# Transposing the last segment on TensorE, and the first input tile in two column parts

## The chip, the cores and the metric

The kernel runs on one core of one Trainium2 chip. The metric is the device time of one execution in microseconds (us), lower is better. A core has five engines that run their own instruction streams in order: PE (TensorE, matmuls and transposes), DVE (VectorE), ACT (ScalarE), POOL (GpSimd) and SP (SyncE, here only a queue that issues transfers). DMA transfers are issued from SP and ACT.

## The reference

The input `x` is 2048 tokens by 640. It is normalized per token, and two branches are computed from the normalized `xn` and combined.

```python
xn = _layernorm(x, axis=-1)
# attention in 4 segments of 512 tokens, 32 heads of 20 columns
q, k, v = (xn @ wq), (xn @ wk), (xn @ wv)          # split in heads and segments
p = softmax(q_s @ k_s.T * scale + causal_mask)      # inside segment s
a_dot = p @ v_s
a_mem = (phi(q_s) @ M) / (phi(q_s) @ z + 1e-6)      # memory of the earlier segments
o = g * a_mem + (1 - g) * a_dot                     # g = sigmoid(beta), one per head
M, z = M + phi(k_s).T @ v_s, z + phi(k_s).sum()     # phi(t) = t + 1 if t > 0 else exp(t)
s = o @ wo
# gated unit
h = sigmoid(xn @ w_gate) * (xn @ w_up)
y = silu(h @ w_down)
out = x + s * y
```

## The kernel before, in words

Tokens are worked on in 4 segments of 512, each of four tiles of 128 tokens (index `j`). Columns come in five chunks of 128 (index `c`, `DC` = 5).

**Order.** The schedule is manual: each engine gets its instructions in the order in which the Python code emits them. A tile from a pool waits until the buffer it gets has been read for the last time. All matmul results other than the scores (`Sps`, four PSUM banks) and the attention sums (`Aps`, one bank) go through one PSUM pool, `ps_d`, of three buffers (line 98), which all helper functions share.

**The head (lines 138 to 186 and 548 to 587).** SP loads the first input tiles, `Wv`, `Wk`, `Wq`. PE runs 11 matmuls on zeros (`keep_warm`). POOL builds constants: the identity `ident` (line 153), ones in `KT` (line 158), then the head indicator `Ind` (lines 160 to 169, six instructions), which `bound_k` (line 290) reads. For each of two pairs of tiles DVE takes statistics (`ln_stats`, lines 203 and 204), POOL turns the variance into a reciprocal root (`ln_rstd`, lines 207 and 208, tile `rs`), and DVE normalizes (`ln_norm`, line 212, tile `xn`). The statistics of both tiles of a pair come before their normalization on DVE. After that `late_constants` (line 174) gives POOL the rest of its constants behind a copy that waits for the fourth normalized tile: ones in `V`, and the block mask `BD`. Then each tile is transposed by PE (`ln_transpose`, line 226, five chunks into one PSUM tile `pT`) and copied by ACT into `xnT` (line 229). ACT issues the loads of `Wg` and `Wu` behind the first and second of these copies (line 573). Projections of V, K and Q follow.

**The middle.** For each unit of attention work PE does scores, ACT exponentials, and between them a planner fills in the rest: every item has a cost in ns, `due` grows by a fixed rate per unit, and `fill` emits items of the queue `dense` (gate, up and down products) until `done` reaches what is due. Items of one segment are planned for fixed slots of the units. Segments 0 to 2 get their attention output `odot` transposed through memory: a spill to `Od` (`out_spill`, line 417), then a DMA transpose to `oT` (line 422), then the output product in `out_mm`.

**The tail (lines 443 to 480 and 749 to 776).** The last segment has 21 units. In slot 18 `tail_spill` writes the first four column chunks of `odot` to memory, in slot 19 `tail_T` reads them back with a DMA transpose. Chunk five depends on the last head group; `tail_T4` transposes it on PE, two tiles at a time, with a copy on ACT (lines 457 and 458). The last attention block of a group is closed by `finalize` (lines 537 to 545, four DVE steps). Two of the eight down products of the last segment are held back (`held`): one is emitted before the last attention block (`held[1]`), one between the output products of tiles 0 and 1 (`held[0]`). A down product (`do_down`, line 409) is evacuated by ACT (tanh, line 412) and DVE (line 413). The eight output pieces are 320 columns wide each: `tail_mm` (line 466), then `tail_out` with a multiplication on DVE (line 473), an addition on POOL for tiles 0 and 1 and on DVE for 2 and 3, and a store.

Of the kernel before, what the change touches and what calls it, by code (L numbers as in the profile page):

```python
# [9 lines left out]
P = 128  # L10
D = 640
H = 32
DH = 20
E1 = DH + 1
NSEG = 4
L = 512
F = 1536
DC = D // P
# [4 lines left out]
HD = D // 2  # L23

BF = mybir.dt.bfloat16
F32 = mybir.dt.float32
ACT = mybir.ActivationFunctionType
ALU = mybir.AluOpType
# [47 lines left out]
def kernel(  # L76
# [14 lines left out]
    nc = tc.nc  # L91
    x2 = A_x.flatten_outer_dims()
    o2 = out.flatten_outer_dims()

    cpool = ctx.enter_context(tc.tile_pool(name="const", bufs=1))
    ps_s = ctx.enter_context(tc.tile_pool(name="ps_s", bufs=1, space=PSUM))
    ps_a = ctx.enter_context(tc.tile_pool(name="ps_a", bufs=1, space=PSUM))
    ps_d = ctx.enter_context(tc.tile_pool(name="ps_d", bufs=3, space=PSUM))
    lnp = ctx.enter_context(tc.tile_pool(name="ln", bufs=2))
# [4 lines left out]
    fpool = ctx.enter_context(tc.tile_pool(name="fpool", bufs=2))  # L104
    xpool = ctx.enter_context(tc.tile_pool(name="xpool", bufs=2))
# [4 lines left out]
    Od = [dpool.tile([L, D], BF, name=f"Od{i}") for i in range(2)]  # L110
# [7 lines left out]
    xt_of, xnT_of = {}, {}  # L118
# [14 lines left out]
    Wo = cpool.tile([P, DC, D], BF, name="Wo")  # L133
# [7 lines left out]
    for half in range(2):  # L141
        load_x(0, ((2 * half, 2 * half + 1), (2 * half + 1, 2 * half + 2)))
        hs = slice(half * HD, (half + 1) * HD)
# [12 lines left out]
    KT = cpool.tile([P, NG, L], BF, name="KT")  # L156
    QT = cpool.tile([P, NG, L], BF, name="QT")
    nc.gpsimd.memset(KT[:].bitcast(mybir.dt.uint32), 0x3F803F80)

    Ind = []  # L160
    for hb in range(2):
        t = cpool.tile([P, 3, 4, 4], F32, name=f"Ind{hb}")
        nc.gpsimd.memset(t[:], -1.0)
        base = 2 * hb * P - 16 * hb * DH
        nc.gpsimd.affine_select(out=t[:], in_=t[:], compare_op=ALU.is_ge, fill=0.0, base=base,
                                pattern=[[P, 3], [-DH, 4], [-4 * DH, 4]], channel_multiplier=1)
        nc.gpsimd.affine_select(out=t[:], in_=t[:], compare_op=ALU.is_ge, fill=0.0, base=DH - 1 - base,
                                pattern=[[-P, 3], [DH, 4], [4 * DH, 4]], channel_multiplier=-1)
        Ind.append(t)

    V = [cpool.tile([P, 4, H, E1], BF, name=f"V{i}") for i in range(2)]
    BD = cpool.tile([P, MOFF[-1]], BF, name="BD")
    Mbd = cpool.tile([P, MOFF[-1]], BF, name="Mbd")
    def late_constants(after):
        nc.gpsimd.tensor_copy(BD[:, 0:1], after[:, 0:1])
        for i in range(2):
            nc.gpsimd.memset(V[i][:, :, :, DH:E1], 1.0)
        nc.gpsimd.memset(BD[:], 1.0)
        for c, (h0, h1) in enumerate(HEADS):
            t = BD[:, MOFF[c]:MOFF[c + 1]].rearrange("p (h e) -> p h e", e=E1)  # L180
            nh, base = h1 - h0 + 1, P * c - DH * h0
            nc.gpsimd.affine_select(out=t, in_=t, compare_op=ALU.is_ge, fill=0.0, base=base,
                                    pattern=[[-DH, nh], [0, E1]], channel_multiplier=1)
            nc.gpsimd.affine_select(out=t, in_=t, compare_op=ALU.is_ge, fill=0.0, base=DH - 1 - base,
                                    pattern=[[DH, nh], [0, E1]], channel_multiplier=-1)
# [24 lines left out]
    def ln_norm(n, j, mv, rs):  # L210
        xn = lnp.tile([P, D], BF, name="xn", bufs=3)
        nc.vector.tensor_scalar(xn[:], xt_of[n][:, j, :], mv[:, j, 0:1], rs[:, j:j + 1],
                                op0=ALU.subtract, op1=ALU.mult)
        return xn
# [6 lines left out]
    def ln_transpose(n, j, xn, eng):  # L221
        if n not in xnT_of:
            xnT_of[n] = xpool.tile([P, DC, L], BF, name="xnT")
        pT = ps_d.tile([P, DC, P], BF, name="pT", tag="d")
        for c in range(DC):
            nc.tensor.transpose(pT[:, c, :], xn[:, c * P:(c + 1) * P], ident[:])
        dst = xnT_of[n][:, :, j * P:(j + 1) * P]
        if eng is nc.scalar:
            nc.scalar.copy(dst, pT[:])  # L229
        else:  # L230
            nc.vector.tensor_copy(dst, pT[:])
# [72 lines left out]
    def bound_dma(n, half, engs):  # L304
        cb = seg[n]["cb", half]
        for r in range(4):
            engs[r % len(engs)].dma_start(QT[32 * r + DH:32 * r + E1, 4 * half:4 * half + 4, :],
                                          cb[4 * r:4 * r + 4, :])
# [116 lines left out]
    def out_store(n, j):  # L425
        tt = 4 * n + j
        nc.sync.dma_start(o2[tt * P:(tt + 1) * P, :], xt_of[n][:, j, :])
# [15 lines left out]
    C4 = (DC - 1) * P  # L443
    tail = {}

    def tail_spill():
        nc.sync.dma_start(Od[(NSEG - 1) % 2][:, 0:C4].rearrange("(j p) d -> p j d", p=P),
                          seg[NSEG - 1]["odot"][:, :, 0:C4])

    def tail_T():  # L450
        tail["oT"] = fpool.tile([P, DC, L], BF, name="oT", bufs=1)
        nc.sync.dma_start_transpose(out=tail["oT"][:, 0:DC - 1, :], in_=Od[(NSEG - 1) % 2][:, 0:C4])

    def tail_T4(j0, j1):
        po = ps_d.tile([P, 2, P], BF, name="po", tag="d")
# [1 line left out]
            nc.tensor.transpose(po[:, j - j0, :], seg[NSEG - 1]["odot"][:, j, C4:D], ident[:])  # L457
        nc.scalar.copy(tail["oT"][:, DC - 1, j0 * P:j1 * P].rearrange("p (j t) -> p j t", t=P), po[:])

    def tail_mm(i, c0, c1):  # L460

        if c0 == 0:
            tail["sp", i] = ps_d.tile([P, HD], F32, name="sp", tag="d")
        j, hs = i // 2, slice((i % 2) * HD, (i % 2 + 1) * HD)
        for c in range(c0, c1):
            nc.tensor.matmul(tail["sp", i][:], lhsT=tail["oT"][:, c, j * P:(j + 1) * P], rhs=Wo[:, c, hs],  # L466
                             start=(c == 0), stop=(c == DC - 1), skip_group_check=True)

    def tail_out(i, eng):
        s = seg[NSEG - 1]  # L470
        j, hs = i // 2, slice((i % 2) * HD, (i % 2 + 1) * HD)
        aa, xr = s["aa"][j], xt_of[NSEG - 1][:, j, :]
        nc.vector.tensor_tensor(aa[:, hs], aa[:, hs], tail["sp", i][:], op=ALU.mult)
        if i >= 6:
            eng.tensor_tensor(xr[:, hs], aa[:, hs], xr[:, hs], op=ALU.add)
            t0 = (4 * NSEG - 1) * P
            nc.sync.dma_start(o2[t0:t0 + P, hs], xr[:, hs])
        elif i % 2:
            eng.tensor_tensor(xr, aa[:], xr, op=ALU.add)
            out_store(NSEG - 1, j)  # L480


    def scores(unit):
# [72 lines left out]
    new_seg(0)  # L556
    xns = {}

    def ln0(j):
        xns[j] = ln_norm(0, j, mv, rs)  # L560

    for pair in range(2):
        for j in (2 * pair, 2 * pair + 1):
            ln_stats(0, j, mv)
            ln_rstd(mv, rs, slice(j, j + 1))
        for j in (2 * pair, 2 * pair + 1):
            ln0(j)
    late_constants(xns[3])
    for j in range(4):
        ln_transpose(0, j, xns[j], nc.scalar)  # L570
        if j < 2:
            w, src = ((Wg, B_w_gate), (Wu, B_w_up))[j]
            load_w(nc.scalar, w, src)
        if j == 0:
            keep_warm(3)
        if j == 1:
            do_V(0, 0, 0, nc.scalar)
            do_V(0, 1, 0, nc.scalar)
        if j == 2:
            do_V(0, 0, 1, nc.scalar)  # L580
            do_V(0, 1, 1, nc.scalar)
            do_V(0, 2, 0, nc.scalar)
# [136 lines left out]
    def fill(want):  # L719
        nonlocal done  # L720
        while done < want and dense and (dense[0][0] < 0 or dense[0][0] in ready):
            _, c, fn = dense.popleft()
            fn()
            done += c
# [8 lines left out]
    for n in range(NSEG):  # L733
        if n >= 1:
            outq.append((n - 1, out_steps(n - 1)))
        for slot, unit in enumerate(units[n]):
            scores(unit)
            pt = exps(unit)
            due += rate
            items = plans[n].get(slot, [])  # L740
            run([it for it in items if it[0] < 600])
            fill(due - rate / 2)
            if pend is not None:
                attend(*pend)
            pend = (n, unit, pt)
            run([it for it in items if it[0] >= 600])
            if outq and downs[outq[0][0]] == 8 and slot >= 5:
                run(outq[0][1].popleft())
                if not outq[0][1]:
                    outq.popleft()  # L750
            if slot == 9:
                ready.add(n + 1)
            if n == NSEG - 1 and slot == len(units[n]) - 3:
                tail_spill()
            if n == NSEG - 1 and slot == len(units[n]) - 2:
                tail_T()
            fill(due)
        if n + 1 < NSEG:
            relayout(n + 1, 1, Kd, KT, nc.sync)
            relayout(n + 1, 1, Qd, QT, nc.sync)  # L760
            bound_dma(n + 1, 1, [nc.sync])
    fill(1e12)
    held[1][2]()
    tail_T4(0, 2)
    attend(*pend)
    for i in range(2):
        tail_mm(i, 0, DC)
        tail_out(i, nc.gpsimd)
    held[0][2]()
    for i in range(2, 4):  # L770
        tail_mm(i, 0, DC)
        tail_out(i, nc.gpsimd)
    tail_T4(2, 4)
    for i in range(4, 8):
        tail_mm(i, 0, DC)
        tail_out(i, nc.vector)

# [1 line left out]
_INS = ['A_x', 'A_wq', 'A_wk', 'A_wv', 'A_wo', 'A_beta', 'B_x', 'B_w_gate', 'B_w_up', 'B_w_down']  # L779
# [26 lines left out]
```

## Time and profile before

| | us |
|---|---|
| median of 3 runs | 343.83 (343.44 to 344.74) |
| the profiled execution | 343.83 |
| its span, first to last instruction | 342.0 |
| costliest group: exponentials on ACT, line 494 | 150.3 busy |
| down products on PE, line 409 | 57.5 busy |
| gate and up products on PE, lines 386 and 395 | 59.7 busy each |
| DMA, bytes moved | 36.45 MB, 107 GB/s mean |

Times in the trace count from the start of the span. The granted TensorE clock is 1.00 over the whole span. An engine's busy time is no measure of what a change is worth: what counts is the wait that ends last at each place, and the chain that ended last follows such waits back from the end. In a row of the timeline the brackets give the engine's idle time before the row and the instruction that ended it. Ends of PE rows are modelled, and rows of independent instructions on one engine can overlap a little.

### The profile page before, as it was taken

How to read it: one execution, taken by the hardware profiler on the slowest of the kernel's cores; microseconds unless marked ns; L12 is line 12 of the kernel's file. 1: busy time of each engine (PE TensorE's matmuls, PEld its weight loads, DVE VectorE, ACT ScalarE, POOL GpSimd, SP SyncE). 2: the span in 40 equal slices, each digit the busy share in tenths (PEclk: the TensorE clock that was granted, in tenths of full speed). 3: DMA queues.
4: the chain of work that ended last, by engine and by line, in shares of the span. 5: the costliest groups of instructions: out<-in, count | busy, mean ns of one | idle time of the engine just before them, and what ended most of it. 6: DMA issues, size and time to landing. Idle time of an engine off the chain costs nothing.

```text
span 342.0 us, 8196 instructions
## 1 busy us (share of the span) xinstructions
PE 333.2 (97%) x3370; PEld 183.6 (54%) x3370; DVE 220.8 (65%) x516; ACT 221.7 (65%) x218; POOL 100.9 (29%) x172
## 2 busy tenths in 40 slices
PE   7999999999999999999999999999999999999995
PEld 3544444665554455556566545556446655544763
DVE  5374374375776777797768875878765575553355
ACT  3523676677786766766786757767965766767620
POOL 6800225223222243223232432232233223232122
PEclk9999999999999999999999999999999999999999
DMA  7987783302246514213265325014144100000132
GB/s 217 378 324 214 147 281 138 80 2 84 86 142 133 154 32 134 55 67 105 74 185 157 79 77 98 21 65 143 37 108 132 27 21 21 20 21 2 58 68 77
DMA packets 51573, 36.45 MB, mean 107 GB/s; under 512 B 27344, under 2 KB 50256, under 8 KB 51536
## 3 DMA queue, kind: packets, MB, share of 16 engines
q1 hardware_dynamic: 50224, 32.00, 33.6%
q10 hardware_dynamic: 1312, 3.93, 2.9%
q8 instruction: 26, 0.43, 0.5%
q14 instruction: 11, 0.09, 0.1%
HBM read 17.05 MB, written 12.32 MB: 86 GB/s over the span
## 4 chain that ended last, share of the span: by engine, by line
PE 86%; DVE 6%; ACT 3%; issue 2%; POOL 2%; ACTq 0%; POOLq 0%
PE yp L409 16%; PE up L395 14%; PE gp L386 14%; PE psq L250 11%; PE Aps L516 9%; PE Sps L486 7%; PE psv L313 5%; PE sp L434 4%; PE am L370 2%; PE cps L299 2%; ACT pt L494 1%; PE dm L351 1%; PE sp L466 1%; ACT mn L330 1%; DVE hT L398 1%
## 5 line engine op out<-in xcount | busy, mean ns | idle before, releaser
L494 ACT ACTIVATE pt<-Sps 128x2048 bf16<-128x2048 f32 (+1 forms) x81 | 150.3, 1855 | 35.7 <-PE Sps L486 33.1
L496 POOL TENSOR_SCALAR_AFFINE_SELECT pt<-pt 128x512 bf16<-128x512 bf16 x128 | 81.5, 652 | 226.0 <-ACT pt L494 226.0
L395 PE MATMUL up<-xnT,Wu 128*128 128x512 bf16 x240 | 59.7, 379 | 1.1 <-ACT tg L389 0.9
L386 PE MATMUL gp<-xnT,Wg 128*128 128x512 bf16 x240 | 59.7, 379 | 0.2 <-ACT V_140 L318 0.2
L409 PE MATMUL yp<-Wd,hT 128*128 128x320 bf16 x384 | 57.5, 299 | 0.0
L398 DVE SCALAR_TENSOR_TENSOR hT<-tg,up 128x512 bf16<-128x512 bf16 x48 | 32.8, 683 | 36.6 <-PE up L395 26.9
L516 PEld LDWEIGHTS <-pt 128*128 128x128 bf16 x1280 | 42.7, 96 | 14.4 <-issue 3.0
L389 ACT ACTIVATE tg<-gp 128x512 bf16<-128x512 f32 x48 | 28.5, 594 | 26.1 <-PE gp L386 26.1
L409 PEld LDWEIGHTS <-hT 128*128 128x128 bf16 x384 | 35.3, 97 | 15.3 <-issue 2.6
L386 PEld LDWEIGHTS <-Wg 128*128 128x128 bf16 x240 | 21.4, 97 | 23.9 <-issue 3.4
L395 PEld LDWEIGHTS <-Wu 128*128 128x128 bf16 x240 | 21.1, 97 | 24.4 <-issue 4.3
L486 PE MATMUL Sps<-QT,KT 21*128 21x128 bf16 (+3 forms) x512 | 32.8, 301 | 0.5 <-ACT pt L494 0.5
L313 PE MATMUL psv<-Wv,xnT 128*128 128x320 bf16 x160 | 26.5, 299 | 0.5 <-DVE ktd L255 0.3
L250 PE MATMUL psq<-xnT,Wq 128*128 128x512 bf16 x100 | 24.3, 378 | 0.0
L250 PE MATMUL psq<-xnT,Wk 128*128 128x512 bf16 x100 | 24.3, 378 | 0.0
L486 PEld LDWEIGHTS <-KT 21*128 21x128 bf16 x512 | 9.7, 92 | 26.9 <-issue 26.4
L516 PE MATMUL Aps<-V_140,pt 128*128 128x21 bf16 x640 | 22.4, 173 | 0.0
L516 PE MATMUL Aps<-V_139,pt 128*128 128x21 bf16 x640 | 22.3, 173 | 0.0
L313 PEld LDWEIGHTS <-xnT 128*128 128x128 bf16 x160 | 15.3, 98 | 10.9 <-ACT xnT L229 0.9
L434 PE MATMUL sp<-Wo,oT 128*128 128x320 bf16 x120 | 20.2, 298 | 0.2 <-ACT tg L389 0.2
L255 DVE CAST ktd<-psq 128x512 bf16<-128x512 f32 x20 | 13.7, 684 | 6.3 <-PE psq L250 6.2
L436 DVE TENSOR_TENSOR aa<-aa,sp 128x320 bf16<-128x320 bf16 x24 | 11.6, 483 | 7.2 <-PE sp L434 7.2
(155 smaller groups left out, 325.4 us busy)
## 6 DMA issues: line engine op xcount, KB each, us to landing
Wg<-in_B_w_gate_dram ACTq DMA_DIRECT2D x1, 1920.0 KB
Wu<-in_B_w_up_dram ACTq DMA_DIRECT2D x1, 1920.0 KB
Wd<-in_B_w_down_dram SPq DMA_DIRECT2D x1, 1920.0 KB
KT<-Kd_92 SPq DMA_DIRECT2D x16, 80.0 KB
QT<-Qd_90 SPq DMA_DIRECT2D x16, 80.0 KB
Xd_95<-xn SPq DMA_DIRECT2D x8, 160.0 KB
KT<-Kd_93 SPq DMA_DIRECT2D x16, 80.0 KB
QT<-Qd_91 SPq DMA_DIRECT2D x16, 80.0 KB
```

Of the source, the lines that this page charges most:

```text
L250: nc.tensor.matmul(ps[:], lhsT=W[:, k, c * P:(c + 1) * P], rhs=xnT_of[n][:, k, :], start=(k == 0), stop=(k == DC - 1))
L313: nc.tensor.matmul(ps[:], lhsT=xnT_of[n][:, k, j * P:(j + 1) * P], rhs=Wv[:, k, half * HD:(half + 1) * HD], start=(k == 0), stop=(k == DC ...
L386: nc.tensor.matmul(gp[:], lhsT=Wg[:, k, f * P:(f + 1) * P], rhs=xnT_of[n][:, k, :], start=(k == 0), stop=(k == DC - 1))
L389: nc.scalar.activation(tg[:], gp[:], ACT.Tanh, scale=0.5)
L395: nc.tensor.matmul(up[:], lhsT=Wu[:, k, f * P:(f + 1) * P], rhs=xnT_of[n][:, k, :], start=(k == 0), stop=(k == DC - 1))
L398: nc.vector.scalar_tensor_tensor(out=h[:], in0=seg[n]["tg"][:], scalar=1.0, in1=up[:], op0=ALU.add, op1=ALU.mult)
L409: nc.tensor.matmul(yp[:], lhsT=s["hT"][f][:, j * P:(j + 1) * P], rhs=Wd[:, f, hs], start=(f == 0), stop=(f == FC - 1))
L434: nc.tensor.matmul(sp[:], lhsT=s["oT"][:, c, j * P:(j + 1) * P], rhs=Wo[:, c, hs], start=(c == 0), stop=(c == DC - 1))
L486: nc.tensor.matmul(Sps[:, r, c0:c0 + ncol], lhsT=KT[32 * r:32 * r + E1, g, kb * P:(kb + 1) * P], rhs=QT[32 * r:32 * r + E1, g, q0:L], star ...
L494: nc.scalar.activation(pt[:, :, 0:ntot], Sps[:, :, 0:ntot], ACT.Exp, scale=SCALE)
L496: nc.gpsimd.affine_select(out=pt[:, :, c0:c0 + P], in_=pt[:, :, c0:c0 + P], compare_op=ALU.is_ge, fill=0.0, base=0, pattern=[[0, 4], [1, P ...
L516: nc.tensor.matmul(acc["ps"][:, qb, r, :], lhsT=t[:, r, off:off + P], rhs=V[n % 2][:, kb, 4 * g + r, :], start=acc["fresh"], stop=True, sk ...
```

## The change

Four edits. Where the whole `Ind` block was built ahead of the first normalization, its six POOL instructions now stand in `late_constants`, behind the copy that waits for the fourth normalized tile. The first input tile is normalized in two column parts (384 and 256), and its transposes are emitted at once, before the second tile's normalization: three chunks copied by ACT, two copied by DVE. For the last segment the spill and the DMA transpose go; the new `tail_T` transposes the four chunks of one tile on PE into a `ps_d` tile and copies 512 columns on ACT (tiles 0 and 2) or DVE (tiles 1 and 3), emitted after the loop over the units and ahead of the held down product. The output pieces of the last tile are 384 and 256 columns wide.

```diff
-    Ind = []
-    for hb in range(2):
-        t = cpool.tile([P, 3, 4, 4], F32, name=f"Ind{hb}")
-        nc.gpsimd.memset(t[:], -1.0)
...
+    Ind = [cpool.tile([P, 3, 4, 4], F32, name=f"Ind{hb}") for hb in range(2)]
...
     def late_constants(after):
         nc.gpsimd.tensor_copy(BD[:, 0:1], after[:, 0:1])
+
+        for hb in range(2):
+            t = Ind[hb]
+            nc.gpsimd.memset(t[:], -1.0)
...
         for i in range(2):
             nc.gpsimd.memset(V[i][:, :, :, DH:E1], 1.0)
...
-    def tail_spill():
-        nc.sync.dma_start(Od[(NSEG - 1) % 2][:, 0:C4].rearrange("(j p) d -> p j d", p=P),
-                          seg[NSEG - 1]["odot"][:, :, 0:C4])
-
-    def tail_T():
-        tail["oT"] = fpool.tile([P, DC, L], BF, name="oT", bufs=1)
-        nc.sync.dma_start_transpose(out=tail["oT"][:, 0:DC - 1, :], in_=Od[(NSEG - 1) % 2][:, 0:C4])
+    def tail_T(j, eng):
+        if j == 0:
+            tail["oT"] = fpool.tile([P, DC, L], BF, name="oT", bufs=1)
+        po = ps_d.tile([P, DC - 1, P], BF, name="po", tag="d")
+        for c in range(DC - 1):
+            nc.tensor.transpose(po[:, c, :], seg[NSEG - 1]["odot"][:, j, c * P:(c + 1) * P], ident[:])
+        dst = tail["oT"][:, 0:DC - 1, j * P:(j + 1) * P]
+        if eng is nc.scalar:
+            nc.scalar.copy(dst, po[:])
+        else:
+            nc.vector.tensor_copy(dst, po[:])
...
+    def tail_piece(j, c0, c1, eng):
+
         s = seg[NSEG - 1]
+        sp = ps_d.tile([P, c1 - c0], F32, name="sp", tag="d")
+        for c in range(DC):
+            nc.tensor.matmul(sp[:], lhsT=tail["oT"][:, c, j * P:(j + 1) * P], rhs=Wo[:, c, c0:c1],
+                             start=(c == 0), stop=(c == DC - 1))
         aa, xr = s["aa"][j], xt_of[NSEG - 1][:, j, :]
+        nc.vector.tensor_tensor(aa[:, c0:c1], aa[:, c0:c1], sp[:], op=ALU.mult)
+        a0 = 0 if c1 == D and j < 3 else c0
+        if j == 3 or c1 == D:
+            eng.tensor_tensor(xr[:, a0:c1], aa[:, a0:c1], xr[:, a0:c1], op=ALU.add)
+            t0 = (4 * (NSEG - 1) + j) * P
+            nc.sync.dma_start(o2[t0:t0 + P, a0:c1], xr[:, a0:c1])
...
+    CA = 3 * P
+
     def ln0(j):
-        xns[j] = ln_norm(0, j, mv, rs)
+        if j:
+            xns[j] = ln_norm(0, j, mv, rs)
+            return
+        xns[0] = lnp.tile([P, D], BF, name="xn", bufs=3)
+        for cs in (slice(0, CA), slice(CA, D)):
+            nc.vector.tensor_scalar(xns[0][:, cs], xt_of[0][:, 0, cs], mv[:, 0, 0:1], rs[:, 0:1],
+                                    op0=ALU.subtract, op1=ALU.mult)
+
+    def first_transpose():
+        xnT_of[0] = xpool.tile([P, DC, L], BF, name="xnT")
+        for c0, c1 in ((0, 3), (3, 5)):
+            pT = ps_d.tile([P, c1 - c0, P], BF, name="pT", tag="d")
+            for c in range(c0, c1):
+                nc.tensor.transpose(pT[:, c - c0, :], xns[0][:, c * P:(c + 1) * P], ident[:])
+            dst = xnT_of[0][:, c0:c1, 0:P]
+            if c0:
+                nc.vector.tensor_copy(dst, pT[:])
+            else:
+                nc.scalar.copy(dst, pT[:])
...
         for j in (2 * pair, 2 * pair + 1):
             ln0(j)
+            if j == 0:
+                first_transpose()
     late_constants(xns[3])
     for j in range(4):
-        ln_transpose(0, j, xns[j], nc.scalar)
+        if j:
+            ln_transpose(0, j, xns[j], nc.scalar)
...
-            if n == NSEG - 1 and slot == len(units[n]) - 3:
-                tail_spill()
-            if n == NSEG - 1 and slot == len(units[n]) - 2:
-                tail_T()
             fill(due)
...
+    for j in range(4):
+        tail_T(j, nc.vector if j % 2 else nc.scalar)
     fill(1e12)
     held[1][2]()
     tail_T4(0, 2)
     attend(*pend)
...
+    tail_piece(0, 0, HD, nc.gpsimd)
+    tail_piece(0, HD, D, nc.gpsimd)
     held[0][2]()
...
+    tail_piece(2, 0, HD, nc.vector)
+    tail_piece(2, HD, D, nc.vector)
+    tail_piece(3, 0, 384, nc.vector)
+    tail_piece(3, 384, D, nc.vector)
```

The old loops over `tail_mm` and `tail_out` at the end go, and the new calls stand in their order: the two pieces of tile 0, the held product, tile 1, the transposes of chunk five for tiles 2 and 3, tile 2, tile 3.

More of the change, by code (lines that the diff above doesn't have):

```diff
@@ L158 @@
     nc.gpsimd.memset(KT[:].bitcast(mybir.dt.uint32), 0x3F803F80)
-    Ind = []
-    for hb in range(2):
-        t = cpool.tile([P, 3, 4, 4], F32, name=f"Ind{hb}")
-        nc.gpsimd.memset(t[:], -1.0)
[L164 to L169, printed above, removed]
+    Ind = [cpool.tile([P, 3, 4, 4], F32, name=f"Ind{hb}") for hb in range(2)]
     V = [cpool.tile([P, 4, H, E1], BF, name=f"V{i}") for i in range(2)]
@@ L175, in late_constants @@
         nc.gpsimd.tensor_copy(BD[:, 0:1], after[:, 0:1])
+        for hb in range(2):
+            t = Ind[hb]
+            nc.gpsimd.memset(t[:], -1.0)
+            base = 2 * hb * P - 16 * hb * DH
+            nc.gpsimd.affine_select(out=t[:], in_=t[:], compare_op=ALU.is_ge, fill=0.0, base=base,
+                                    pattern=[[P, 3], [-DH, 4], [-4 * DH, 4]], channel_multiplier=1)
+            nc.gpsimd.affine_select(out=t[:], in_=t[:], compare_op=ALU.is_ge, fill=0.0, base=DH - 1 - base,
+                                    pattern=[[-P, 3], [DH, 4], [4 * DH, 4]], channel_multiplier=-1)
         for i in range(2):
@@ L458, in tail_T4 @@
         nc.scalar.copy(tail["oT"][:, DC - 1, j0 * P:j1 * P].rearrange("p (j t) -> p j t", t=P), po[:])
[L460 to L469, printed above, removed]
+    def tail_piece(j, c0, c1, eng):
         s = seg[NSEG - 1]
-        j, hs = i // 2, slice((i % 2) * HD, (i % 2 + 1) * HD)
+        sp = ps_d.tile([P, c1 - c0], F32, name="sp", tag="d")
+        for c in range(DC):
+            nc.tensor.matmul(sp[:], lhsT=tail["oT"][:, c, j * P:(j + 1) * P], rhs=Wo[:, c, c0:c1],
+                             start=(c == 0), stop=(c == DC - 1))
         aa, xr = s["aa"][j], xt_of[NSEG - 1][:, j, :]
[L473 to L480, printed above, removed]
+        nc.vector.tensor_tensor(aa[:, c0:c1], aa[:, c0:c1], sp[:], op=ALU.mult)
[4 more added lines that the diff above has]
+            nc.sync.dma_start(o2[t0:t0 + P, a0:c1], xr[:, a0:c1])
     def scores(unit):
@@ L765 @@
     attend(*pend)
-    for i in range(2):
-        tail_mm(i, 0, DC)
-        tail_out(i, nc.gpsimd)
+    tail_piece(0, 0, HD, nc.gpsimd)
+    tail_piece(0, HD, D, nc.gpsimd)
     held[0][2]()
-    for i in range(2, 4):
-        tail_mm(i, 0, DC)
-        tail_out(i, nc.gpsimd)
+    tail_piece(1, 0, HD, nc.gpsimd)
+    tail_piece(1, HD, D, nc.gpsimd)
     tail_T4(2, 4)
-    for i in range(4, 8):
-        tail_mm(i, 0, DC)
-        tail_out(i, nc.vector)
+    tail_piece(2, 0, HD, nc.vector)
+    tail_piece(2, HD, D, nc.vector)
+    tail_piece(3, 0, 384, nc.vector)
+    tail_piece(3, 384, D, nc.vector)
 _INS = ['A_x', 'A_wq', 'A_wk', 'A_wv', 'A_wo', 'A_beta', 'B_x', 'B_w_gate', 'B_w_up', 'B_w_down']
```

## The prediction

> **What bounds the kernel now.** First the page: its first part and the chain that ended last.
>
> ```profile
> PE 333.2 (97%) x3370; PEld 183.6 (54%) x3370; DVE 220.8 (65%) x516; ACT 221.7 (65%) x218; POOL 100.9 (29%) x172
> ...
> PE 86%; DVE 6%; ACT 3%; issue 2%; POOL 2%; ACTq 0%; POOLq 0%
> ```
>
> PE (TensorE) holds 86% of the chain. The reader is to see that outside a short head and a short tail nothing is worth anything unless PE starts earlier, stalls longer or does more. So I read the timeline at both ends, in order of time: start, duration, engine, line, tile, idle time before it. First the head:
>
> ```profile
> 4.01 0.21 DVE L204 BATCH_NORM_AGGREGATE mv<-st 128x2 f32<-128x12 f32 x1
> ...
> 4.55 0.32 POOL L167 TENSOR_SCALAR_AFFINE_SELECT Ind_135<-Ind_135 128x48 f32<-128x48 f32 x1
> ...
> 4.85 0.23 POOL L207 TENSOR_SCALAR rs<-mv 128x1 f32<-128x1 f32 x1
> 5.00 0.21 DVE L204 BATCH_NORM_AGGREGATE mv<-st 128x2 f32<-128x12 f32 x1
> ...
> 5.78 0.45 DVE L212 TENSOR_SCALAR xn<-xt_111,mv,rs 128x640 bf16<-128x640 bf16 x1 [0.57 <-POOL rs L208]
> ...
> 6.70 0.45 DVE L212 TENSOR_SCALAR xn<-xt_111,mv,rs 128x640 bf16<-128x640 bf16 x1 [0.47 <-POOL rs L208]
> ...
> 9.69 0.45 PE L226 MATMUL pT<-ident,xn 128*128 128x128 bf16 x5 [0.39 <-DVE xn L212]
> ```
>
> The first tile's statistics end at 4.22, yet POOL takes up `rs` at 4.85, behind the head indicator `Ind`. VectorE (DVE) waits for `rs` twice (0.57 and 0.47 us), and each later DVE step follows. At 9.69 PE still waits for DVE; from there PE runs almost without a gap.
>
> Then the tail:
>
> ```profile
> 328.26 0.44 ACT L412 ACTIVATE t_5149<-yp 128x320 bf16<-128x320 f32 x1 [0.60 <-PE yp L409]
> ...
> 328.46 1.79 PE L409 MATMUL yp<-Wd,hT 128*128 128x320 bf16 x12
> 328.73 0.49 DVE L413 SCALAR_TENSOR_TENSOR aa<-t_5149,yp 128x320 bf16<-128x320 bf16 x1 [1.47 <-ACT t_5149 L412]
> 329.13 0.20 DVE L537 RECIPROCAL rd<-Aps 128x8 f32<-128x8 f32 x1
> ...
> 329.93 0.24 DVE L545 TENSOR_TENSOR odot<-odot,od 128x160 bf16<-128x160 bf16 x1
> ...
> 330.23 0.28 PE L457 MATMUL po<-ident,odot 128*128 128x128 bf16 x2
> ...
> 330.62 0.37 ACT L458 COPY oT<-po 128x256 bf16<-128x256 bf16 x1
> ```
>
> PE goes from one matmul group to the next and never waits for the transposed `oT`; the chain stays on PE until 336.70 and then on DVE until 339.24. DVE is occupied without a break from 328.73 to 330.17: evacuation of the sixth down product, then four steps of `finalize`.
>
> **What the Trainium skill says.** "PSUM — Partial Sum Buffer", "PSUM: the matmul accumulator": matmul results leave PE only through PSUM, in 2 KiB banks. So a PE transpose costs a buffer and a copy as well; the trace agrees (`po` and `pT` each have an ACT copy behind them). "TensorE: Matmul & The Clock Gate", "Wait — 56ns, not 53.3ns?": 55.6 ns start to start for 128 columns, warm. The trace agrees: five transposes last 0.45 us, two 0.28, so 0.057 each and 0.17 fixed. "VectorE: DVE Perf Modes", "The TRN2 errata" and "The perf-mode tier table": a copy out of PSUM takes 120 + columns/mode cycles at 0.96 GHz, and 16-bit data may go at up to 2 per cycle. The trace has the fp32 case only (512 columns 0.685 us against 0.658 by the formula) and no bf16 PSUM read on DVE.
>
> **The head.** Six POOL instructions of `Ind` (3.09 to 4.87, 1.78 us) go behind the copy at 10.86, ahead of the `V` and `BD` memsets. POOL's constants then end near 18.6 instead of 16.8; its next work is at 36.62. `Ind` is first read on DVE at 20.02 and 25.67 and would be built by about 12.7; `V` ones are read from 39.35. All hidden. If this cover were gone, DVE's `ik` would wait by the excess.
>
> First `rs`: in the second pair it takes 0.97 us from `mv` end (8.18) to ready (9.15). So 4.22 + 0.97 = 5.19; DVE is free at 5.21; norm starts about 5.23 instead of 5.78. In two parts it costs 0.31 to 0.38 and 0.25 to 0.35 (bounds: all of the 0.446 us row that is not a fixed 0.11 goes with columns, or fixed is 0.28), the second starting 0.08 before the first's end as independent DVE rows do: part two ends 5.71 to 5.88. Its two transposes (0.28, 0.05 after it) end at 6.04 to 6.21, behind part one's three, which end by 6.0. Now DVE's own copy of 256 columns stands in front of the second tile's norm: it starts at 6.08 to 6.25 and lasts 0.28 at 2 per cycle (256/2/0.96 + 150 ns) or 0.42 at 1. The second `rs` is ready at 5.21 + 0.97 = 6.18. So the second norm starts at 6.28 to 6.59 against 6.70: gain 0.1 to 0.4, I take 0.3. From there statistics, norms and transposes of tiles 3 and 4 follow on DVE with unchanged durations, so PE's 9.69 becomes about 9.4. The part-one copy on ACT (384 columns, 0.48 by ACT's 0.37 for 256 and 0.69 for 640) ends before `psv` needs it.
>
> ACT issues the `Wg` load behind its first copy, so about 0.8 us earlier (6.78 to 6.0); `Wu` follows. They share the DMA engines with `Wq`. By bytes moved per queue, SP's loads of x, Wv, Wk and Wq (3.1 MB) are in by about 15; 0.8 us earlier sharing could delay the end by about 1 us, and `Wq` is used at 17.68. Hidden: cost 0; without cover, the lateness beyond 17.4.
>
> **The tail.** Removed: a spill (issue 0.38 us) and a DMA transpose (2.40) on SP. The next SP work is the output at 334.50 and PE didn't wait for `oT`, so this gives nothing. Added: 16 transposes in four groups, each with a buffer of the three-deep pool and a 512-column copy, ACT, DVE, ACT, DVE. They stand on PE just ahead of the held down product that started at 328.46. By themselves 16 x 0.057 = 0.91 us.
>
> But the buffers: group 0 starts at 328.46, its ACT copy (512 columns, 0.585 as the fp32 row) runs 328.90 to 329.49. Group 1 starts at 328.69. Group 2 needs the sixth down product's buffer, free after DVE's 328.73 + 0.49 = 329.22: PE 329.27 to 329.67; ACT copy to 330.29. Group 3 takes group 0's buffer at 329.54. Group 1's copy waits on DVE behind `finalize`: start about 330.08, 0.42 us at 2 per cycle (512/2/0.96 + 150 ns), end 330.50. The fourth tile after it in the rotation, the held down product, starts at 330.55. Loss: 330.55 - 328.46 = 2.09 us. Behind the waiting matmul stand the rest of PE's program: last attention, all output products. These are in the old order, with group 3's copy (done by 331) and `finalize` before them, so nothing gives the loss back. A pause of this length does not slow PE: at 248.48 it resumed after 0.91 us idle with five matmuls in 1.24 as before.
>
> Price bounds: DVE copy at 1 per cycle 0.685, start 330.82, loss 2.36. If the buffer handed to the down product is group 2's, freed by ACT at 330.29, the loss is 1.88. The trace shows that the rotation isn't strict: at 224.65 a `psv` waits for a `ktd` copy and starts while the older `gp` is still being read until 225.01.
>
> The last output pieces become 384 and 256 columns instead of 320 twice. DVE's multiplications and additions cover the same 640 columns with the same counts, and DVE is what ends last there, so its end stays at 339.24 plus the shift. The last store is 64 KB instead of 80; 0 to 0.1 us gain out of 2.76 after 339.24, taken as 0.
>
> **Sum.** -0.3 + 2.09 = +1.79 us. The profiled execution took 343.83 with a span of 342.0 and 1.83 around it; its time equals the median of the three runs. Forecast 343.83 + 1.79 = 345.6.
>
> **Rivals.**
> 1. The down product gets the buffer freed by ACT: 1.88 - 0.35 = +1.5, 345.3, which is not slower by this study's bound (0.5%, 1.72 us, is about what a measurement can tell from no change, so slower begins at 345.55). It decides as soon as that buffer is free before 330.45. For it: ACT is idle from 328.70. Against: a strict rotation, which most groups show by never waiting, gives group 1's. 0.32.
> 2. DVE copies bf16 from PSUM at 1 per cycle, or the product gets group 3's buffer: +2.36 - 0.15 = +2.2, 346.0, up to 346.6 with group 3. For it: all PSUM rows on DVE run at 1. Against: the skill's tier table. 0.19.
> 3. The earlier `Wg` load makes `Wq` late enough to stall the projections: more than 2.7 us late is needed to cost anything; each further us adds one, 346.5. Against: the byte counts. 0.04.
> 4. PE gains more than the head shows, because buffers in the long middle fall otherwise; the trace's waits for buffers there sum to about 2 us. With all of them gone 343.6; beyond that nothing speaks for faster. 0.05.
>
> The forecast case has 0.40. Its own range is 345.1 to 346.0, slightly more of it above 345.55 than below. Slower: 0.23 of it, 0.19 of rival 2, 0.04 each of rivals 1 and 3: 0.50. Same: 0.17 + 0.28 + 0.01 = 0.46. Faster 0.04. Range for 8 in 10: 344.7 to 346.5.
>
> **What would show it.** Head: `rs` starts near 4.3, the second norm near 6.4, PE's third-tile transposes near 9.4. Tail: groups of four transposes near 328.2, a DVE copy of 512 columns of 0.42 behind `finalize`, and an idle time of about 0.6 us on PE ended by that copy before the seventh down product. Wrong if PE runs into that product without a gap, if the DVE copy comes ahead of `finalize`, or if the K and Q projections wait for DMA.

## The result and the profile after

The changed kernel takes 345.25 us (median of 6 runs, 345.0 to 345.53) against 343.86 for the kernel before (6 runs): +1.39 us, a ratio of 1.0038 with a 95% interval of 1.0025 to 1.0051. By the bound that the prediction names, 345.55 us, this counts as the same time and not as slower. The profiled execution took 345.33 us with a span of 343.5.

First the page of the changed kernel, busy times and the chain's shares by engine:

```profile
PE 334.4 (97%) x3386; PEld 184.5 (54%) x3386; DVE 222.7 (65%) x520; ACT 222.7 (65%) x220; POOL 100.3 (29%) x172
...
PE 87%; DVE 6%; ACT 4%; issue 2%; ACTq 0%
```

POOL, 2% of the chain before, has left it; ACT has grown from 3 to 4%. PE has 16 more instructions, the transposes. The page can't say what that is worth, so again both ends in order of time. The head of the changed kernel:

```profile
4.31 0.23 POOL L205 TENSOR_SCALAR rs<-mv 128x1 f32<-128x1 f32 x1 [1.16 <-DVE mv L202]
...
5.24 0.64 DVE L562 TENSOR_SCALAR xn<-xt_111,mv,rs 128x384 bf16<-128x384 bf16 x2
...
6.26 0.29 DVE L573 COPY xnT<-pT 128x256 bf16<-128x256 bf16 x1 [0.38 <-PE pT L570]
6.47 0.44 DVE L210 TENSOR_SCALAR xn<-xt_111,mv,rs 128x640 bf16<-128x640 bf16 x1
...
9.45 0.45 PE L224 MATMUL pT<-ident,xn 128*128 128x128 bf16 x5 [0.39 <-DVE xn L210]
```

POOL takes up `rs` at 4.31 (4.85 before), the second normalization starts at 6.47 (6.70), and PE's transposes of the third tile at 9.45 (9.69): 0.24 us earlier. The copy at 6.26 stands between the two normalizations.

The tail of the changed kernel:

```profile
328.37 0.61 PE L449 MATMUL po<-ident,odot 128*128 128x128 bf16 x8
...
328.79 0.59 ACT L452 COPY oT<-po 128x512 bf16<-128x512 bf16 x1 [0.19 <-PE po L449]
...
329.17 0.63 PE L449 MATMUL po<-ident,odot 128*128 128x128 bf16 x8 [0.20 <-DVE aa L411]
...
329.59 0.59 ACT L452 COPY oT<-po 128x512 bf16<-128x512 bf16 x1 [0.22 <-PE po L449]
329.83 0.24 DVE L540 TENSOR_TENSOR odot<-odot,od 128x160 bf16<-128x160 bf16 x1
329.99 0.75 DVE L454 COPY oT<-po 128x512 bf16<-128x512 bf16 x2
330.23 1.79 PE L407 MATMUL yp<-Wd,hT 128*128 128x320 bf16 x12 [0.42 <-ACT oT L452]
```

Two groups of transposes run at once, the third waits for the evacuation of the sixth down product (DVE, 0.20 idle), and the held down product starts 0.42 us after the fourth group, released by ACT's second copy, which ends at 329.59 + 0.59 = 330.18. It started at 328.46 before. The two DVE copies of 512 columns come behind `finalize`.

To see where else time went, I take one row that both traces have 81 times, the exponentials on ACT, and compare their starts with those of before. They show three steps and then the tail:

| stretch | changed kernel minus before, us |
|---|---|
| third tile's transposes, 9.69 before | -0.24 |
| first exponential, 34.68 before | -0.57 |
| exponentials up to 221 | -0.56 to -0.58 |
| exponentials from 227 to the last, 326.64 before | -0.09 to -0.11 |
| held down product, 328.46 before | +1.77 |
| end of DVE's last row, 339.24 before | 340.66 + 0.29 - 339.24 = +1.71 |
| end of the span, 342.0 before | +1.5 |

So the tail alone costs 1.71 + 0.10 = 1.81 us on DVE. Two things in the middle, where nothing was changed, are as large as the head's gain: 0.33 us won at the first scores and 0.47 lost near 224. The first scores, one row from each kernel. Before:

```profile
33.81 0.83 PE L486 MATMUL Sps<-QT,KT 21*128 21x512 bf16 x4
```

After:

```profile
33.48 0.59 PE L481 MATMUL Sps<-QT,KT 21*128 21x512 bf16 x4
```

The same four matmuls last 0.39 to 0.40 us elsewhere (307.69 in before, for one). Here 0.43 and 0.19 us of wait are hidden inside the row, between its matmuls, where no idle time is printed (in before the four start over a stretch of 0.5 us). They read the rows of `QT` that the last small transfers of the head, `QT<-cb`, bring. The loss near 224, before:

```profile
222.66 1.83 POOL L496 TENSOR_SCALAR_AFFINE_SELECT pt<-pt 128x512 bf16<-128x512 bf16 x2 [2.53 <-ACT pt L494]
222.68 0.49 DVE L329 TENSOR_SCALAR mn<-ktok 128x1280 bf16<-128x1280 bf16 x1
...
224.65 0.84 PE L313 MATMUL psv<-Wv,xnT 128*128 128x320 bf16 x5 [0.31 <-DVE ktd L255]
```

After:

```profile
222.09 1.48 POOL L491 TENSOR_SCALAR_AFFINE_SELECT pt<-pt 128x512 bf16<-128x512 bf16 x2 [2.52 <-ACT pt L489]
222.11 0.96 DVE L327 TENSOR_SCALAR mn<-ktok 128x1280 bf16<-128x1280 bf16 x1
...
224.56 0.84 PE L311 MATMUL psv<-Wv,xnT 128*128 128x320 bf16 x5 [0.79 <-DVE ktd L253]
```

A POOL and a DVE row start 0.02 us apart in both kernels. In the first POOL is stretched (1.83), in the second DVE (0.96), and PE waits 0.79 in place of 0.31 for what DVE does next. "GPSIMD Engine Reference" of the Trainium skill, in its specifications, calls POOL's SBUF interfaces shared with VectorE; the two rows fit that, though no run here shows who is served first or why.

### The profile page after: what moved, and what is told of

The parts are those of the page before. It is cut to its first block, busy times and chain, and to the rows that moved or that the text cites. A ratio compares the mean times of both kernels' runs of the same rounds, so it can differ in the third digit from the quotient of the medians.

```text
span 343.5 us, 8233 instructions
## 1 busy us (share of the span) xinstructions
PE 334.4 (97%) x3386; PEld 184.5 (54%) x3386; DVE 222.7 (65%) x520; ACT 222.7 (65%) x220; POOL 100.3 (29%) x172
## 4 chain that ended last, share of the span: by engine, by line
PE 87%; DVE 6%; ACT 4%; issue 2%; ACTq 0%
PE yp L407 16%; PE up L393 14%; PE gp L384 13%; PE psq L248 11%; PE Aps L511 8%; PE Sps L481 7%; PE psv L311 5%; PE sp L432 4%; PE am L368 2%; PE cps L297 2%; ACT pt L489 1%; PE wps L547 1%; PE sp L467 1%; PE dm L349 1%; ACT mn L328 1%
```

## The experiments

Theory on the tail: besides PE's own transposes, the loss holds a wait for PSUM buffers, which copies end. Rival: transposes and copies cost that much wherever they are and however buffers fall. Theory on the head: its gain reaches PE but is lost or not by transfers. Rival: it is worth its 0.25 us. Exponentials are compared with those of the profiled kernel before; each kernel has one profile. "Tail" is the end of DVE's last row minus 339.24, less the offset of the last exponential (in `tail_early`, whose transposes begin ahead of that one, of the exponential before it).

| kernel | median, us | ratio to before, 95% | first exponential | last | tail |
|---|---|---|---|---|---|
| head_only | 344.19 | 1.0005 (0.9994 to 1.0017) | +0.12 | +0.60 | -0.01 |
| tail_only | 345.39 | 1.0041 (1.0029 to 1.0053) | -0.45 | -0.54 | 1.82 |
| narrow_only | 344.08 | 1.0001 (0.9991 to 1.0010) | +0.03 | +0.49 | 0.07 |
| spare_banks | 348.27 | 1.0121 (1.0098 to 1.0145) | +0.71 | +1.08 | 3.45 |
| wide_groups | 345.11 | 1.0030 (1.0018 to 1.0043) | +1.29 | +1.66 | 0.85 |
| tail_early | 345.96 | 1.0048 (1.0034 to 1.0063) | +1.17 | +1.54 | 1.80 |
| x1_late | 343.76 | 0.9985 (0.9975 to 0.9994) | -0.45 | -0.08 | |
| head_x1_late | 343.93 | 0.9994 (0.9981 to 1.0007) | -0.59 | -0.68 | |
| wg_early | 344.27 | 1.0003 (0.9992 to 1.0015) | -0.03 | +0.43 | |
| head_wg | 343.77 | 0.9994 (0.9985 to 1.0002) | +1.06 | +1.05 | |
| head_wg_x1 | 343.49 | 0.9981 (0.9974 to 0.9988) | -0.25 | -0.35 | |
| ind_wg_x1 | 343.08 | 0.9976 (0.9966 to 0.9986) | -0.83 | -0.93 | |

**The parts alone.** `head_only` is the changed kernel with the old tail, `tail_only` the old kernel with the new tail. Both are put together from the code of the two kernels, unchanged.

> The head of the change alone (Ind later, first tile in two parts), tail of before. Theory A, the head gains twice: 0.25 us on DVE's chain and 0.3 us more at the first scores, because the earlier Wg and Wu loads are out of the way of the spills; part of it can be lost again where a POOL select and a DVE step of phi meet near 222 us. Then exponentials run 0.57 us earlier from the first on, and the time is 0.1 to 0.6 us under before: 343.3 to 343.8. Rival, the head is worth only what the normalization chain shows: 0.25 us earlier everywhere, first scores as in before. Sum check: with the tail costing 1.5, head plus tail must give the change's +1.4.

> The tail of the change alone (PE transposes and narrower last pieces), head of before. If the parts add: seventh down product 1.87 us later than in before, DVE's last row 1.8 later, last store 0.2 shorter, so +1.6 us against before (345.4). Rival, the head is what costs (a collision started by its shift): then this stays under +1.2.

The tail alone gives +0.41% (345.39 - 343.91 = 1.48 us), the whole of the result; the head alone gives nothing that can be measured. The tail's loss is the same with either head, 1.81 and 1.82, as `tail_only` was expected to show. In the head alone the chain did gain (third tile's transposes at 9.50, with x arriving 0.05 later), but PE then stood at the first scores, and this time the idle time is printed:

```profile
33.95 0.81 PE L484 MATMUL Sps<-QT,KT 21*128 21x512 bf16 x4 [0.35 <-DMA QT<-cb]
```

They end at 34.76, against 33.81 + 0.83 = 34.64 in before. Theory A expected a second gain there; in this execution the place took the first one away. Both expectations of `head_only` miss: the start and the length of the first scores differ from one execution to the next, with the transfers that they wait for. (`tail_only`, with the head of before, had its first scores in 0.40 us.)

**narrow_only**: before with the new widths of the last tile's pieces (the calls; the helper is that of the changed kernel).

```diff
-    for i in range(4, 8):
-        tail_mm(i, 0, DC)
-        tail_out(i, nc.vector)
+    tail_piece(2, 0, HD, nc.vector)
+    tail_piece(2, HD, D, nc.vector)
+    tail_piece(3, 0, 384, nc.vector)
+    tail_piece(3, 384, D, nc.vector)
```

> Before with the last tile's two output pieces 384 and 256 columns wide, nothing else. Theory: DVE's last row ends where it did (within 0.05 us), the last store takes 0.2 us less, -0.2 us in the span (341.8). Rival: the store's time does not depend on its width; no change of the span, and the 0.2 us seen in the change has another cause.

No gain: the ratio is 1.0001. DVE's end is 0.07 later than its offset explains, and from there to the end of the span it takes 2.70 us, against 2.76 in before and 2.55 in the changed kernel. So the 0.2 us seen there is not to be had by the width alone; where it comes from stays open.

**spare_banks**: the groups go into the banks of the scores.

```diff
-        po = ps_d.tile([P, DC - 1, P], BF, name="po", tag="d")
+        po = Sps[:, j, :].bitcast(BF)[:, 0:(DC - 1) * P].rearrange("p (c t) -> p c t", t=P)
```

> The changed kernel with its four groups of transposes in the banks of Sps, which nobody reads after the last exponentials, in place of buffers of the shared pool; same transposes, same copies. Theory, buffers: without the shared pool the transposes run in one piece and the seventh down product follows 0.9 us after them, against 1.87 in the change; the end comes 0.9 us earlier than in the change (344.3 to 344.4). Rival, the copies and the transposes themselves are the cost: no change against the changed kernel, 345.2.

Neither was met; it became slower by 3.0 us than the changed kernel (348.27 - 345.25). In the profiles 1.64 us of the difference are in the tail (3.45 against 1.81), and nearly all the rest lies ahead of it. The timeline of this kernel, its second to fourth group and one copy on DVE:

```profile
330.61 0.38 PE L449 MATMUL Sps<-ident,odot 128*128 128x128 bf16 x4 [0.67 <-ACT oT L452]
...
331.17 0.42 DVE L454 COPY oT<-Sps 128x512 bf16<-128x512 bf16 x1
...
331.64 0.38 PE L449 MATMUL Sps<-ident,odot 128*128 128x128 bf16 x4 [0.65 <-DVE oT L454]
...
332.70 0.38 PE L449 MATMUL Sps<-ident,odot 128*128 128x128 bf16 x4 [0.67 <-ACT oT L452]
```

Each group waits until the copy of the group before is done, although each has a bank of its own. The reading that fits is that the four banks are one tile here, and that the waits fall between its writes and reads as a whole; no run tests it. So this experiment put in more waits and says nothing on the theory.

**wide_groups** asks the same question in another way: two groups of eight.

```diff
-        po = ps_d.tile([P, DC - 1, P], BF, name="po", tag="d")
-        for c in range(DC - 1):
-            nc.tensor.transpose(po[:, c, :], seg[NSEG - 1]["odot"][:, j, c * P:(c + 1) * P], ident[:])
+        po = ps_d.tile([P, DC - 1, 2, P], BF, name="po", tag="d")
+        for i in range(2):
+            for c in range(DC - 1):
+                nc.tensor.transpose(po[:, c, i, :], seg[NSEG - 1]["odot"][:, j + i, c * P:(c + 1) * P], ident[:])
...
-    for j in range(4):
-        tail_T(j, nc.vector if j % 2 else nc.scalar)
+    tail_T(0, nc.scalar)
+    tail_T(2, nc.vector)
```

> The changed kernel with its 16 transposes in two groups of eight (two shared buffers in place of four; one copy of 1024 columns on ACT, one on DVE). Same transposes, same columns copied. Theory, buffers: the seventh down product gets the buffer of the sixth, free before the transposes end, so PE has no idle time before it; tail loss against before about 0.95 us in place of 1.81, time about 0.9 under the changed kernel (344.4). Rival, the copies themselves must be waited for: loss stays at 1.8 or grows, since the DVE copy (two bf16 columns per cycle, about 0.7 us) then ends later than the copies of the change.

Its timeline:

```profile
330.13 1.05 PE L450 MATMUL po<-ident,odot 128*128 128x128 bf16 x16
...
330.77 1.01 ACT L453 COPY oT<-po 128x1024 bf16<-128x1024 bf16 x1 [0.41 <-PE po L450]
...
331.02 1.79 PE L407 MATMUL yp<-Wd,hT 128*128 128x320 bf16 x12
...
331.75 0.68 DVE L455 COPY oT<-po 128x1024 bf16<-128x1024 bf16 x1
```

All 16 transposes run in one piece and the down product follows with no idle time, while one copy still runs and the other hasn't begun. The tail's loss is 0.85 in place of 1.81, so the rival falls: neither copy has to be waited for. Of the 1.81 us, 0.85 are PE's transposes, and 0.96 come from waits for buffers. In the changed kernel's trace 0.62 of this is printed as idle time (0.20 + 0.42). The rest fits what a wait costs beyond its idle time: a row of transposes has 0.17 us that doesn't depend on their number (0.45 for five, 0.28 for two); in `wide_groups` the down product's row begins 0.16 before the modelled end of the row ahead of it, and ahead of a wait that overlap is lost, here twice.

This is the reading of one profile. The median is only 0.14 under the changed kernel's, with times from 344.22 to 347.31; the fastest is 0.78 under the changed kernel's fastest (345.0). The profiled execution, at 346.14 one of the longest, had another wait in the head, seen in the waits of this kernel (total, times, longest, us):

```profile
PE psq L248 <- DMA Wq<-in_A_wq_dram: 1.7, 1, 1.7
```

**tail_early**: four groups, two at the end of slot 19, two in slot 20 behind the scores.

```diff
+            if n == NSEG - 1 and slot == len(units[n]) - 1:
+                for j in range(2, 4):
+                    tail_T(j, nc.vector if j % 2 else nc.scalar)
...
+            if n == NSEG - 1 and slot == len(units[n]) - 2:
+                for j in range(2):
+                    tail_T(j, nc.vector if j % 2 else nc.scalar)
             fill(due)
...
-    for j in range(4):
-        tail_T(j, nc.vector if j % 2 else nc.scalar)
```

> The changed kernel with the transposes of tiles 0 and 1 emitted at the end of slot 19 and those of tiles 2 and 3 in slot 20 behind its scores, where DVE isn't in finalize and down products lie between. Theory, place and buffers: PE's waits for these buffers go or shrink; tail loss 0.9 to 1.2 us in place of 1.81, time 344.3 to 344.6. Rival: the shared pool of three is short there too and the waits only move; loss 1.6 or more, 345.1.

Here this experiment's own rival is right: the loss is 1.80, as much as in the change, and the waits only moved. The timeline:

```profile
326.02 0.61 PE L449 MATMUL po<-ident,odot 128*128 128x128 bf16 x8
...
326.95 1.79 PE L407 MATMUL yp<-Wd,hT 128*128 128x320 bf16 x12 [0.32 <-DVE aa L411]
...
328.89 0.62 PE L449 MATMUL po<-ident,odot 128*128 128x128 bf16 x8
...
329.78 1.79 PE L407 MATMUL yp<-Wd,hT 128*128 128x320 bf16 x12 [0.27 <-DVE aa L411]
```

PE waits twice, as in the change: 0.32 and 0.27 us, where it was 0.20 and 0.42, and each time for the evacuation of the down product that was in flight. At both places two more buffers in a row use up the pool of three. A larger pool was not run.

**The first scores.** `x1_late` moves one load of 640 KB out of the way of the `QT<-cb` transfers, `head_x1_late` does the same with the new head.

```diff
-    load_x(1)
     bound_k(0, 0)
...
     spill(0, 1, nc.sync, nc.sync)
+    load_x(1)
```

> Before with the load of the second segment's input (640 KB) issued behind the second spill in place of ahead of the four QT<-cb transfers that the first scores need. Theory: the end of the first scores is set by those transfers; they are issued 0.5 us earlier and have less traffic beside them, the first scores take 0.40 us without a wait in place of 0.83, and the first exponential is 0.3 to 0.45 us earlier; time -0.3 to -0.5 us (343.5). Rival: the first scores wait for the relayouts of K and Q, which this leaves alone; no change.

> The head of the change with the same later load, tail of before. Theory: with the wait at the first scores gone, the 0.25 us that the normalization chain gains reaches the first exponential: 0.55 to 0.7 us earlier than in before, 0.25 earlier than in the kernel with the later load alone; time 343.2. Rival: the head's gain is lost again at the first scores as in the head alone; then both kernels with the later load have the same first exponential.

In both the first scores last 0.40 us, and the first exponential is 0.45 and 0.59 us earlier. One such profile proves little: `tail_only`, which leaves the load where it was, has the same -0.45; the transfers ahead of these, `QT<-Qd`, were issued at 26.0 in it (26.6 in before). What all the profiles show is this: every kernel with the later load issues `QT<-cb` 1.5 to 1.6 us after `QT<-Qd` and has no wait at the first scores (four of four). The seven others that had no wait for `Wq`, the subject of the next part, issue it 1.9 to 2.0 us after, and six of them wait. With the head of before the later load gives 343.76, a ratio of 0.9985. With the new head the profile shows 0.14 us more, less than the 0.25 expected, because the head's chain gained only that much here: the third tile's transposes are at 9.54. In this execution the first tile's transposes start at 5.87 (5.68 in the changed kernel), behind the matmuls of `keep_warm`, and DVE's copy and the second normalization follow them. The median doesn't show a gain: 343.93, with runs from 343.1 to 346.0 where those with the old head stay in 343.28 to 344.53.

**The Wq wait.** Kernels with the new head waited for `Wq` in three of six profiles (spare_banks 0.8, wide_groups 1.7, tail_early 1.6 us), and those with the old head, tail_only, narrow_only, x1_late and before, in none of four. ACT issues `Wg` at 6.06 in the changed kernel, which had no such wait, and at 6.78 in before. `wg_early` makes only this load early, `head_wg` makes both loads late with the new head.

```diff
+            if j == 0:
+                tick = cpool.tile([P, 1], F32, name="tick")
+                nc.scalar.copy(tick[:], rs[:, 0:1])
+                load_w(nc.scalar, Wg, B_w_gate)
...
-        if j < 2:
-            w, src = ((Wg, B_w_gate), (Wu, B_w_up))[j]
-            load_w(nc.scalar, w, src)
+        if j == 1:
+            load_w(nc.scalar, Wu, B_w_up)
```

> Before with only the Wg load issued earlier: ACT issues it behind a copy of one column of rs, near 5.8 us instead of 6.78; head and tail otherwise as in before. Theory, the load: Wg then takes bandwidth from Wq as it does in kernels with the new head, PE waits 0.5 to 2 us for Wq near 17.9 in part or all of the executions, and the times spread up to 2 us above before (median 344.3 to 345.5). Rival, the wait for Wq has nothing to do with this load: times and spread as in before (343.9).

```diff
-        if j < 2:
-            w, src = ((Wg, B_w_gate), (Wu, B_w_up))[j]
-            load_w(nc.scalar, w, src)
+        if j == 1:
+            load_w(nc.scalar, Wg, B_w_gate)
+            load_w(nc.scalar, Wu, B_w_up)
```

> The new head with the Wg and Wu loads both issued behind the second tile's copy (about 7.5 us, later than in before), tail of before. Theory, the load: PE never waits for Wq, the spread shrinks to that of before or less; the later end of Wu makes the first spill and with it the first scores wait more (0.5 us or so), so the median stays at 343.6 to 344.2. Rival: the wait for Wq stays in some executions, times up to 345 and more.

`wg_early` issued the load at 5.78. No matmul waited for `Wq`, and its 14 times stay in 343.66 to 344.79. But PE's weight load did wait for it, 0.27 us, until 17.83, just before the matmuls needed it; before shows no such wait. So an early load was not shown to cost time by itself, yet it does make `Wq` late. The bytes say the same for all the profiles. By 14 us SP's queue, which brings x, `Wv`, `Wk` and `Wq`, had moved 2.90 to 3.06 of 3.12 MB in the seven kernels that issue `Wg` at 5.78 to 6.48, and 3.07 to 3.12 in the seven that issue it at 6.76 or later; `wg_early`, the earliest, has the least. As it has the old head, and `head_wg` and `head_wg_x1` with late loads have the new one, it is the load that counts and not the head. With the new head and the loads at 7.45 and 7.93 (`head_wg`) no wait for `Wq` was seen, and the first scores waited instead:

```profile
34.88 0.83 PE L484 MATMUL Sps<-QT,KT 21*128 21x512 bf16 x4 [1.34 <-DMA QT<-cb]
```

What the issue time doesn't explain is which executions wait: the three that did issued `Wg` at 6.02, 6.29 and 6.48, the three of the new head that didn't at 6.06, 6.12 and 6.24. That part stays open; it would take several profiles of one kernel.

**Versions that beat both kernels.** `head_wg_x1` joins the two edits, the later `Wg` and `Wu` loads and the later input load, with the new head; `ind_wg_x1` has the same two edits and of the new head only the later `Ind`, with the first tile in one part. Both have the tail of before.

> The same with the second segment's input loaded behind the second spill. Theory: neither Wq nor the first scores wait, the 0.25 us of the head's chain arrives: first exponential 0.5 to 0.7 us earlier than in before, median 343.3 to 343.6, spread under 1 us, under before and under the later load alone (343.76). Rival: the first scores still wait, 343.8 or more.

> Of the new head only the later Ind, first tile in one part as in before; Wg and Wu loads behind the second tile's copy, the second segment's input behind the second spill. Theory: the second normalization starts when its rs is ready (6.35 to 6.4) rather than behind a DVE copy (6.47), so the chain gains 0.3 against 0.25 with the split; median 343.3 to 343.6, not slower than with the split. Rival: the split is needed and this gives back the gain, 343.7 or more.

Both are faster than before by about 0.2%: ratios 0.9981 and 0.9976, 343.49 and 343.08 us, with a spread of about 1 us and less, and both intervals stay under 1. The split isn't needed. DVE in the second:

```profile
5.12 0.45 DVE L211 TENSOR_SCALAR xn<-xt,mv,rs 128x640 bf16<-128x640 bf16 x1
6.30 0.45 DVE L211 TENSOR_SCALAR xn<-xt,mv,rs 128x640 bf16<-128x640 bf16 x1 [0.74 <-POOL rs L207]
```

The second normalization starts when its `rs` is ready, no copy stands ahead of it, and PE is at the third tile at 9.29, the earliest of all these kernels. Part of that is x coming 0.12 us earlier in this execution: the first `mv` starts at 3.89 (4.01 in before), so the chain's own gain is 0.40 - 0.12 = 0.28. In `head_wg_x1`'s profile the split even cost time: DVE's copy waited until 6.69 for PE, whose matmuls of `keep_warm` ran until about 6.1 by their modelled end, and the second normalization started at 6.90, later than in before (6.70).

## Why the prediction was right, and where not

The forecast was +1.79 us, 345.6; measured +1.39, 345.25, inside the range. That it came so near owes something to luck: the head's gain was put at 0.3 and did not show in the time (`head_only`, 1.0005), the tail's loss at 2.09 and was 1.48 by itself (`tail_only`), and the two errors offset each other in part. The prediction gave slower, from 345.55 on, a chance of 0.50 and same 0.46; the measured time lies 0.30 us under that bound.

**The tail's mechanism was right, the buffer was not.** Spill and DMA transpose gave nothing back, the four groups stand where expected, the third waits for the sixth down product (PE at 329.17), DVE's copies come behind `finalize`. A DVE copy of 512 bf16 columns takes 0.42 us (331.17 in `spare_banks`), as priced at 2 columns per cycle, and one of 1024 takes 0.68 (`wide_groups`); so the doubled price of rival 2 falls. The step that failed is "the fourth tile after it in the rotation": the down product got the buffer that ACT frees, which is rival 1. Its price was put at 1.88; measured it is 1.77 + 0.10 = 1.87. On DVE's last row 1.81 is left. The note that the rotation isn't strict was the right warning, though nothing shown ahead of the run decided between the two buffers.

**The tail's floor** of 0.91 us for 16 transposes was right as well: in `wide_groups` the held down product is 331.02 - 328.46 - 1.66 = 0.90 us later, and 0.85 are left at DVE's last row.

**The head's -0.3** had the right size for the DVE chain (0.24) and the wrong reach. "PE runs almost without a gap" from there on was the mis-read line: the row at 33.81 hides 0.43 us of wait. A gain ahead of a wait for transfers can be lost there, and in `head_only` none was measured.

**The Wg load at cost 0** held in the changed kernel's profile and was wrong as a certainty. Rival 3 named the wait for `Wq`, and three profiles of kernels with the new head show it, at 0.8 to 1.7 us. The earlier load does slow SP's transfers, as the bytes show; why only some executions then wait stays open.

**Later constants on POOL** were hidden, as said: `Ind` is built at 12.5 (12.21 + 0.32), read near 20.

**The narrow pieces at 0**: no effect was measured, 1.0001 (0.9991 to 1.0010).

In the profiled execution the sum is 0.24 gained in the head, 0.33 gained and 0.47 lost in the middle, 1.81 lost in the tail and 0.21 gained behind it (2.55 against 2.76 us), +1.50 in all. That it is below the forecast comes from the buffer (2.09 forecast, 1.81 left at DVE's end) and from the shorter stretch behind, which the forecast took as 0.

## What to carry to other kernels

A transfer that no engine waits for has nothing to give back, so moving its work to the engine that bounds the kernel can only add; here even the best form that was run adds 0.85 us. When an edit puts new tiles into a small shared pool just ahead of a long product, write down for each buffer who frees it and when: by the profiles half of the loss was the wait for buffers, and fewer, wider tiles removed it. Before counting a gain at the start of a kernel, look for a row that takes longer than its likes: a wait inside a group of matmuls is not printed as idle time, and a gain ahead of it may stop there.

## What was not expected of the hardware

POOL and DVE rows that start 0.02 us apart seem to share a delay that falls to either: the DVE `mn` row near 222 us takes 0.48 to 0.49 us in 6 of 14 profiles, and 0.96 in 8, in kernels that are the same up to there too (before and narrow_only). The POOL row is then 1.83 in the first six and 1.47 or 1.48 in the others, and PE starts its next projection about 0.47 us later in the second case. That is more than most edits of the head were worth, so a single trace must not be used to price such an edit by its span.
